# Run-time expert tiles of a MoE kernel: order of turns, down products and weight splits written by hand

## The chip, the cores and the metric

One core of a Trainium2 chip runs the whole program. The metric is the device time of one execution in microseconds (us). TensorE does matrix products and transposes into PSUM, ScalarE and VectorE copy and compute between PSUM and SBUF, GpSimd issues the indirect transfers (gathers and scatters), SyncE issues the others.

## The reference

Three layers in sequence, in float32. Attention with rotary embedding (batch 4, 8 heads, 576 rows, head width 64); a dense layer with a SoLU activation and a layer norm (512 to 1024 to 512); and a routed layer, which is the one that matters here:

```
do_compute = (x @ w_skip) > 0            # 2304 rows of 512
e_idx  = argmax(x @ w_gate)              # 8 experts
h      = maximum(x @ w1[e], 0)           # 512 -> 1024
y      = gate_w * (h @ w2[e])            # 1024 -> 512
out    = x + y where do_compute, else x
```

## The kernel before, in words

Every float32 product is made of three products of split operands: a high part `h` and a low part `l` of each operand, as `hh`, `hl`, `lh`. So a product of a 128-row tile with a 512-wide half of `w1` is 4 row blocks (`kc`) x 3 = 12 matmuls of 128 x 512 (`up_mm`, L1077), both halves 24, and the product with `w2` is 8 blocks x 3 = 24 matmuls into one PSUM tile `ops` (`dn_mm`, L1098).

Attention, the dense layer, the routing and the first two expert tiles (`NEAR = 2`, of one expert that is chosen early) are put in order by a planner: a list scheduler with costs and priorities, whose result `g.emit` writes under a manual schedule. This part is the same in both kernels.

The other expert tiles come in a loop that is unrolled for the largest possible number of tiles (`NTL`), each iteration inside a run-time condition on the tile count (`n_t > t`, L1276). With these inputs six run; the texts call them the first to the sixth (last) dynamic tile; `u = t + 2` numbers all expert tiles. Rows sorted by expert are gathered 128 at a time. One iteration of the loop has these steps:

- `up_mm` and `relu` for each half `hf`: twelve matmuls into `hp`, then ScalarE writes `hs` (L1081).
- `gmeta(u + 3)`, `gather(u + 2)`: GpSimd asks for the row numbers (L1048) and the rows (L1058) of later tiles.
- `xp_t`, `xp_h`, `xp_l`: four transposes (L1065) of the next tile's rows, a high-part copy on ScalarE (L1068) and a low part on VectorE (L1071).
- a turn of each half of `hs`: four transposes (`tn_t`, L1085) into a `tp` tile, the high part `hh` on ScalarE (`tn_h`, L1088), the low part `hl` on VectorE (`tn_l`, L1092).
- 24 down products, `finish` (VectorE, `ys`, L1101) and `put` (GpSimd, the scatter to `out`, L1104).

Where a tile is the first of another expert, its weights are split. They have been loaded into `w1r` and `w2r` by SyncE; `split1` writes `w1h` (ScalarE, L966) and `w1l` (VectorE, L967) for one of 4 blocks of 128 x 1024, `split2` does `w2h` (L970) and `w2l` (L971) likewise. `change(t, parts)` loads a flag of the table `ct` into a register of each engine concerned and does this under a run-time condition (L1265, L1266); part 1 is w1, part 2 is w2 with `fetch` of the next expert's weights. The texts call such a condition a gate: load of the flag, compare-and-branch, the block, a jump. With these inputs only the fourth dynamic tile changes the expert. In the loop of before no manual schedule is set, so within an iteration the framework's scheduler decides where each engine's instructions go.

Of the kernel before, what the change touches and what calls it, by code (L numbers as in the profile page):

```python
# [264 lines left out]
def kern(ctx, tc, q, k, v, w_in, w_out, g_ln, w_skip, w_gate, w1, w2, cs, ids, out):  # L265
    nc = tc.nc
    P = 128
# [7 lines left out]
    KC = DM // P  # L275
    FC = FF // P
# [11 lines left out]
    half = cst.tile([P, 1], F32, name="half")  # L288
# [674 lines left out]
    m = {}  # L963

    def split1(kc, raw):
        nc.scalar.activation(m["w1h"][:, kc], raw, AF.Copy)  # L966
        nc.vector.tensor_tensor(m["w1l"][:, kc], raw, m["w1h"][:, kc].bitcast(F32), op=ALU.subtract)  # L967

    def split2(kc, raw):
        nc.scalar.activation(m["w2h"][:, kc:kc + 2], raw, AF.Copy)  # L970
        nc.vector.tensor_tensor(m["w2l"][:, kc:kc + 2], raw, m["w2h"][:, kc:kc + 2].bitcast(F32), op=ALU.subtract)  # L971
# [73 lines left out]
    def gmeta(u):  # L1045
        mt = m["mt"][u % 5]
        r = erw[:, u:u + 1] if u < NEAR else m["rows"][:, u - NEAR:u - NEAR + 1]
        nc.gpsimd.indirect_dma_start(out=mt, out_offset=None, in_=srt[:, :],  # L1048
                                     in_offset=bass.IndirectOffsetOnAxis(ap=r, axis=0),
                                     bounds_check=E * REG - 1, oob_is_err=False)  # L1050
# [5 lines left out]
    def gather(u):  # L1056
        src, top = (out[0:2 * S], 2 * S) if u < NEAR else (out, NT)
        return nc.gpsimd.indirect_dma_start(  # L1058
            out=m["xr"][u % 3], out_offset=None, in_=src[:, :],
            in_offset=bass.IndirectOffsetOnAxis(ap=m["mt"][u % 5][:, 1:2].bitcast(I32), axis=0),  # L1060
            bounds_check=top - 1, oob_is_err=False)

    def xp_t(u, tp):
        for k_ in range(KC):
            nc.tensor.transpose(tp[:, k_ * P:(k_ + 1) * P], m["xr"][u % 3][:, k_ * P:(k_ + 1) * P], ident)  # L1065

    def xp_h(u, tp):
        nc.scalar.activation(m["xh"][u % 2], tp, AF.Copy)  # L1068

    def xp_l(u, tp):  # L1070
        nc.vector.tensor_tensor(m["xl"][u % 2], tp, m["xh"][u % 2].bitcast(F32), op=ALU.subtract)  # L1071

    def up_mm(u, hf, kc, h):
        xh, xl = m["xh"][u % 2], m["xl"][u % 2]
        fs, ks = slice(hf * 512, hf * 512 + 512), slice(kc * P, kc * P + P)
        for y, (a, bb) in enumerate(((xh, "w1h"), (xh, "w1l"), (xl, "w1h"))):
            nc.tensor.matmul(h, lhsT=a[:, ks], rhs=m[bb][:, kc, fs], start=(kc == 0 and y == 0),  # L1077
                             stop=(kc == KC - 1 and y == 2))

    def relu(hf, h):  # L1080
        nc.scalar.activation(m["hs"][:, hf * 512:hf * 512 + 512], h, AF.Relu)  # L1081

    def tn_t(hf, tp):
        for k_ in range(4):
            nc.tensor.transpose(tp[:, k_ * P:(k_ + 1) * P], m["hs"][:, (4 * hf + k_) * P:(4 * hf + k_ + 1) * P], ident)  # L1085

    def tn_h(hf, tp):
        nc.scalar.activation(m["hh"][:, hf * 512:hf * 512 + 512], tp, AF.Copy)  # L1088

    def tn_l(hf, tp):  # L1090
        fs = slice(hf * 512, hf * 512 + 512)
        nc.vector.tensor_tensor(m["hl"][:, fs], tp, m["hh"][:, fs].bitcast(F32), op=ALU.subtract)  # L1092

    DOWN = [(a, bb, kc) for a, bb in (("hh", "w2h"), ("hh", "w2l"), ("hl", "w2h")) for kc in range(FC)]

    def dn_mm(i, ob):
        a, bb, kc = DOWN[i]
        nc.tensor.matmul(ob, lhsT=m[a][:, kc * P:kc * P + P], rhs=m[bb][:, kc], start=(i == 0), stop=(i == len(DOWN) - 1))  # L1098

    def finish(u, ob):  # L1100
        nc.vector.scalar_tensor_tensor(m["ys"][u % 2], ob, m["mt"][u % 5][:, 0:1], m["xr"][u % 3], op0=ALU.mult, op1=ALU.add)  # L1101

    def put(u):
        nc.gpsimd.indirect_dma_start(  # L1104
            out=out, out_offset=bass.IndirectOffsetOnAxis(ap=m["mt"][u % 5][:, 1:2].bitcast(I32), axis=0),
            in_=m["ys"][u % 2], in_offset=None, bounds_check=NT - 1, oob_is_err=False)
# [96 lines left out]
    for kc in range(KC):  # L1203
        for hf in range(2):
            i = 2 * kc + hf
# [24 lines left out]
    for u in range(NEAR):  # L1230
        x = 102 + 10 * u
# [12 lines left out]
    rows, ct = m["rows"], m["ct"]  # L1244

    def fetch(reg, after=None):
        for i in range(2):
            d = [nc.sync.dma_start(m["w1r"][:, 2 * i:2 * i + 2], w1v(reg & (E - 1))[:, 2 * i:2 * i + 2], cond=reg < SL)]
            d += [nc.sync.dma_start(m["w2r"][:, 4 * i:4 * i + 4], w2v(reg & (E - 1))[:, 4 * i:4 * i + 4], cond=reg < SL)]
            if after is not None:  # L1250
                for x in d:
                    tc.add_manual_dep(x.ins, after.ins.name, mybir.DependencyInfo(mybir.DependencyClass.Sync, mybir.DependencyReason.DATA), reason="rows first")
# [6 lines left out]
    hps = [[pm.tile([P, 512], F32, name=f"hp{i}{j}") for j in range(2)] for i in range(2)]  # L1259
    tps = [pm.tile([P, 512], F32, name=f"tp{i}") for i in range(3)]  # L1260
    ops = pm.tile([P, 512], F32, name="ops")

    def change(t, parts):
        engs = [mybir.EngineType.Activation, mybir.EngineType.DVE] + [mybir.EngineType.SP] * (parts >> 1)
        new = nc.values_load(ct[0:1, 0, t:t + 1], engines=engs, min_val=0, max_val=1)  # L1265
        with tc.If(new > 0):  # L1266
            if parts & 1:
                for kc in range(KC):
                    split1(kc, m["w1r"][:, kc])
            if parts & 2:  # L1270
                for kc in range(0, FC, 2):
                    split2(kc, m["w2r"][:, kc:kc + 2])
                fetch(nc.sync.value_load(ct[0:1, 1, t:t + 1], min_val=0, max_val=SL))

    change(0, 3)
    with ExitStack() as nest:  # L1276
        for t in range(NTL):
            nest.enter_context(tc.If(n_t > t))
            u = t + NEAR
            if t:  # L1280
                change(t, 2)
            for hf in range(2):
                for kc in range(KC):
                    up_mm(u, hf, kc, hps[u % 2][hf])
                relu(hf, hps[u % 2][hf])
            gmeta(u + 3)
            gather(u + 2)
            xp_t(u + 1, tps[0])
            xp_h(u + 1, tps[0])
            xp_l(u + 1, tps[0])  # L1290
            for hf in range(2):
                tn_t(hf, tps[1 + hf])
                tn_h(hf, tps[1 + hf])
                tn_l(hf, tps[1 + hf])
            if t + 1 < NTL:
                change(t + 1, 1)
            for i in range(len(DOWN)):
                dn_mm(i, ops)
            finish(u, ops)
            put(u)  # L1300

# [41 lines left out]
```

## Time and profile before

| | us |
|---|---|
| median of 3 runs | 689.01 (686.5 to 692.22) |
| profiled execution | 688.96 |
| its span | 687.2 |
| TensorE busy | 634.6 (92%) |
| VectorE busy | 483.7 (70%) |
| ScalarE busy | 372.7 (54%) |
| GpSimd busy | 259.6 (38%) |

The span is the time from the first to the last instruction that the profiler saw in one execution; 1.76 us of that execution lie around it. Busy shares are averages over stages with different limits. The loop of dynamic tiles takes the stretch from 593.84 to 677.15 us of the span, 83.31 us. Starts and ends of matmuls overlap because they are pipelined; the step from one start to the next is the time that one costs.

### The profile page before, as it was taken

What the parts mean: (1) busy time and instruction counts of PE and PEld (TensorE: products, weight loads), DVE (VectorE), ACT (ScalarE), POOL (GpSimd) and SP (SyncE); (2) the same over time, 40 slices, a digit from 0 to 9 for tenths busy, and PEclk for the clock granted to TensorE, in tenths of its full rate; (3) what the DMA queues carried; (4) which work ended last, traced back from release to release, by engine and by line L of the source; (5) the groups of instructions that cost most, each with busy time, mean ns of one, the idle gap of its engine ahead of it and who ended that gap; (6) DMA issues with size and microseconds to landing.
All of it is one profiled execution on the core that took longest, in us unless ns stands there. A gap on an engine that the chain in (4) does not pass through costs nothing. (4 is left out here: it accounts for less than half of the span.)

```text
span 687.2 us, 12857 instructions
## 1 busy us (share of the span) xinstructions
PE 634.6 (92%) x4588; PEld 483.6 (70%) x4588; DVE 483.7 (70%) x1199; ACT 372.7 (54%) x899; POOL 259.6 (38%) x278
## 2 busy tenths in 40 slices
PE   2597989989999999999999999999999989898993
PEld 1465766767777787777777777777877767677772
DVE  5588798898678788687886975868569857124411
ACT  2687798776557575854556754565335421123321
POOL 5776369463343633243333243112020422321330
PEclk9998999989999999999999999999999999999998
DMA  4633344431212331124222012100134211541000
GB/s 129 169 98 114 85 143 144 116 96 62 64 36 65 83 84 34 38 65 81 69 37 64 12 36 50 35 17 1 22 108 117 78 46 26 188 151 32 18 32 11
DMA packets 42187, 49.10 MB, mean 71 GB/s; under 512 B 27508, under 2 KB 27636, under 8 KB 42112
## 3 DMA queue, kind: packets, MB, share of 16 engines
q1 hardware_dynamic: 39744, 44.43, 24.3%
q0 software_dynamic: 2368, 3.74, 1.8%
q8 instruction: 38, 0.62, 0.4%
q14 instruction: 37, 0.30, 0.1%
HBM read 38.50 MB, written 6.99 MB: 66 GB/s over the span
## 5 line engine op out<-in xcount | busy, mean ns | idle before, releaser
L624 ACT ACTIVATE P<-S,nm 128x576 f32<-128x576 f32 x144 | 106.7, 742 | 45.5 <-DVE nm L621 44.2
L621 DVE TENSOR_REDUCE nm<-S 128x1 f32<-128x576 f32 x144 | 106.8, 748 | 12.3 <-PE S L618 11.6
L847 PE MATMUL A<-woh,lh 128*128 128x512 f32 x288 | 108.0, 416 | 0.0
L618 PE MATMUL S<-k,qa 64*128 64x288 f32 x576 | 96.5, 322 | 5.3 <-ACT P L624 3.2
L724 PE MATMUL T<-ptall,vt 128*64 128x256 f32 (+2 forms) x960 | 92.9, 337 | 0.8 <-DVE qa L558 0.8
L685 PE MATMUL T<-ident,P 128*128 128x128 f32 x576 | 87.9, 285 | 5.9 <-ACT ptall L692 2.0
L647 POOL TENSOR_SCALAR P<-P,sr 128x576 f32<-128x576 f32 x57 | 45.8, 809 | 111.2 <-DVE sr L633 94.7
L618 PE MATMUL S<-k,qb 64*128 64x288 f32 x384 | 81.4, 333 | 5.1 <-ACT P L624 5.1
L685 PEld LDWEIGHTS T<-ident,P 128*128 128x128 f32 x576 | 67.6, 145 | 24.2 <-issue 6.9
L618 PEld LDWEIGHTS S<-k,qa 64*128 64x128 f32 x576 | 70.4, 192 | 17.7 <-ACT P L624 6.5
L724 PEld LDWEIGHTS T<-ptall,vt 128*64 128x64 f32 (+1 forms) x960 | 55.7, 138 | 30.9 <-issue 6.5
L692 ACT ACTIVATE ptall<-T 128x512 f32<-128x512 f32 (+1 forms) x110 | 51.2, 491 | 37.2 <-PE T L685 36.8
L618 PEld LDWEIGHTS S<-k,qb 64*128 64x128 f32 x384 | 57.3, 196 | 16.6 <-ACT P L624 7.6
L847 PEld LDWEIGHTS A<-woh,lh 128*128 128x128 f32 x288 | 54.4, 189 | 12.3 <-issue 2.1
L772 PE MATMUL S<-wih,xth 128*128 128x512 f32 x144 | 60.7, 422 | 0.1
L772 PE MATMUL S<-wih,xtl 128*128 128x512 f32 x144 | 56.6, 393 | 0.0
L847 PE MATMUL A<-wol,lh 128*128 128x512 f32 x144 | 56.5, 392 | 0.0
L772 PE MATMUL S<-wil,xth 128*128 128x512 f32 x144 | 56.3, 391 | 0.0
L498 POOL TENSOR_TENSOR rt<-raw,csq 128x576 f32<-128x576 f32 x24 | 34.8, 1452 | 55.2 <-PE T L529 36.1
L694 DVE COPY ptall<-T 128x512 f32<-128x512 f32 (+1 forms) x82 | 44.2, 552 | 11.8 <-PE T L685 11.3
L801 POOL TENSOR_TENSOR st<-st,half 128x1 f32<-128x1 f32 x18 | 10.7, 595 | 79.6 <-DVE st L798 47.0
L923 POOL DMA_INDIRECT srt<-gi,ix x18 | 19.5, 1085 | 55.1 <-DVE sc L893 13.7
(228 smaller groups left out, 1302.3 us busy)
## 6 DMA issues: line engine op xcount, KB each, us to landing
qb<-qa SPq DMA_DIRECT2D x30, 256.0 KB, 3.8
raw<-in_q SPq DMA_DIRECT2D x16, 288.0 KB, 3.2
raw<-in_k SPq DMA_DIRECT2D x16, 288.0 KB, 3.1
out<-xs SPq DMA_DIRECT2D x36, 128.0 KB, 2.7
s<-in_moe_w_in SPq DMA_DIRECT2D x8, 512.0 KB, 4.9
s<-in_moe_w_out SPq DMA_DIRECT2D x8, 512.0 KB, 3.4
st<-in_moe_w SPq DMA_DIRECT2D x8, 512.0 KB, 3.7
w1r<-in_moe_w SPq DMA_DIRECT2D x4, 1024.0 KB, 8.0
```

Source lines behind the costliest of these rows:

```text
L498: e.tensor_tensor(t1[:, 0:NJ].rearrange("p j (e i) -> p j e i", e=2), raw.t.rearrange("p j (e i) -> p j e i", e=2), c, op=ALU.mult)
L618: nc.tensor.matmul(sp[:, bank, 0:288], lhsT=l, rhs=r_, start=first, stop=fin)
L621: nc.vector.tensor_reduce(nm[:, x:x + 1], sp.t[:, :, 0:288], AX.XY, ALU.max, negate=True)
L624: nc.scalar.activation(pt[:, x * S:(x + 1) * S].rearrange("p (a b) -> p a b", a=2), sp.t[:, :, 0:288], AF.Exp, bias=nm[:, x:x + 1], accum_ ...
L647: nc.gpsimd.tensor_scalar(y, y, sr[:, x:x + 1], 1.0, op0=ALU.mult, op1=ALU.mult)
L685: nc.tensor.transpose(tp.t[:w_, (y - g0) * P:(y - g0) * P + P], pt[:, y * P:y * P + w_], ident)
L692: nc.scalar.activation(ov, iv, AF.Copy)
L694: nc.vector.tensor_copy(ov, iv)
L724: nc.tensor.matmul(xp.t[64 * h:64 * h + 64, 0:M], lhsT=l, rhs=r_, start=(i == 0), stop=(i == 4))
L772: nc.tensor.matmul(hp[:, hf], lhsT=a, rhs=bb, start=(kc == 0 and y == 0), stop=(kc == KC - 1 and y == 2))
L847: nc.tensor.matmul(ob.t, lhsT=lh[:, a, kc], rhs=bb[:, kc], start=(kc == 0 and y == 0), stop=(kc == FC - 1 and y == 2))
L923: nc.gpsimd.indirect_dma_start(out=srt[:, :], out_offset=bass.IndirectOffsetOnAxis(ap=ix[:, 0:1], axis=0), in_=gi.t, in_offset=None, bound ...
```

## The change

The loop gets a manual schedule, so each engine's instructions stand in the order in which the code lists them. The first turn stands inside the second up product, after two of its four row blocks. The down products are listed with the four blocks of `hh` and `hl` from the first half first (12 products), then the other 12; four of them stand ahead of the second turn, the rest behind it. The split of w1 for the next tile stands behind the second turn, and that of w2 in two blocks, one ahead of the first up product and one behind the first relu; each block has a gate of its own, with one flag load per tile.

```diff
--- before.py
+++ after.py
@@ -1260,42 +1260,64 @@
     tps = [pm.tile([P, 512], F32, name=f"tp{i}") for i in range(3)]
     ops = pm.tile([P, 512], F32, name="ops")
 
-    def change(t, parts):
-        engs = [mybir.EngineType.Activation, mybir.EngineType.DVE] + [mybir.EngineType.SP] * (parts >> 1)
-        new = nc.values_load(ct[0:1, 0, t:t + 1], engines=engs, min_val=0, max_val=1)
-        with tc.If(new > 0):
-            if parts & 1:
-                for kc in range(KC):
-                    split1(kc, m["w1r"][:, kc])
-            if parts & 2:
-                for kc in range(0, FC, 2):
-                    split2(kc, m["w2r"][:, kc:kc + 2])
+    AD = [mybir.EngineType.Activation, mybir.EngineType.DVE, mybir.EngineType.SP]
+    new = {}
+
+    def change1(t):
+        new[t] = nc.values_load(ct[0:1, 0, t:t + 1], engines=AD, min_val=0, max_val=1)
+        with tc.If(new[t] > 0):
+            for kc in range(KC):
+                split1(kc, m["w1r"][:, kc])
+
+    def change2(t, half):
+        with tc.If(new[t] > 0):
+            for kc in range(4 * half, 4 * half + 4, 2):
+                split2(kc, m["w2r"][:, kc:kc + 2])
+            if half:
                 fetch(nc.sync.value_load(ct[0:1, 1, t:t + 1], min_val=0, max_val=SL))
 
-    change(0, 3)
-    with ExitStack() as nest:
+
+    first = [i for i in range(len(DOWN)) if DOWN[i][2] < 4]
+    order = first + [i for i in range(len(DOWN)) if DOWN[i][2] >= 4]
+    AHEAD = 4
+
+    def down(part):
+        for x in part:
+            a, bb, kc = DOWN[x]
+            nc.tensor.matmul(ops, lhsT=m[a][:, kc * P:kc * P + P], rhs=m[bb][:, kc], start=(x == order[0]),
+                             stop=(x == order[-1]))
+
+    def turn(hf):
+        tn_t(hf, tps[1 + hf])
+        tn_h(hf, tps[1 + hf])
+        tn_l(hf, tps[1 + hf])
+
+    change1(0)
+    with tc.manual_schedule(), ExitStack() as nest:
         for t in range(NTL):
             nest.enter_context(tc.If(n_t > t))
             u = t + NEAR
-            if t:
-                change(t, 2)
-            for hf in range(2):
-                for kc in range(KC):
-                    up_mm(u, hf, kc, hps[u % 2][hf])
-                relu(hf, hps[u % 2][hf])
+            change2(t, 0)
+            for kc in range(KC):
+                up_mm(u, 0, kc, hps[u % 2][0])
+            relu(0, hps[u % 2][0])
+            change2(t, 1)
+            for kc in range(KC // 2):
+                up_mm(u, 1, kc, hps[u % 2][1])
+            turn(0)
+            for kc in range(KC // 2, KC):
+                up_mm(u, 1, kc, hps[u % 2][1])
+            relu(1, hps[u % 2][1])
             gmeta(u + 3)
             gather(u + 2)
             xp_t(u + 1, tps[0])
             xp_h(u + 1, tps[0])
             xp_l(u + 1, tps[0])
-            for hf in range(2):
-                tn_t(hf, tps[1 + hf])
-                tn_h(hf, tps[1 + hf])
-                tn_l(hf, tps[1 + hf])
+            down(order[:AHEAD])
+            turn(1)
             if t + 1 < NTL:
-                change(t + 1, 1)
-            for i in range(len(DOWN)):
-                dn_mm(i, ops)
+                change1(t + 1)
+            down(order[AHEAD:])
             finish(u, ops)
             put(u)
 
```

TensorE, second dynamic tile, from the last up product on. `hp_6593` is the second half's PSUM tile, `tp_6594` that of the next rows, `tp_6595` and `tp_6596` those of the two turns. Before:

```order
L1077 MATMUL hp_6593<-w1h,xl_6095 128x512
L1065 MATMUL tp_6594<-ident,xr_6104 128x128
L1266 UNCONDITIONAL_BRANCH
L1065 MATMUL tp_6594<-ident,xr_6104 128x128 x3
L1085 MATMUL tp_6595<-ident,hs 128x128 x4
L1085 MATMUL tp_6596<-ident,hs 128x128 x4
L1098 MATMUL ops<-w2h,hh 128x512 x8
L1098 MATMUL ops<-w2l,hh 128x512 x8
L1098 MATMUL ops<-w2h,hl 128x512 x8
```

Now, from the last product of the second row block of the second half on:

```order
L1077 MATMUL hp_6593<-w1h,xl_6095 128x512
L1085 MATMUL tp_6595<-ident,hs 128x128 x4
L1077 MATMUL hp_6593<-w1h,xh_6093 128x512
L1077 MATMUL hp_6593<-w1l,xh_6093 128x512
...
L1077 MATMUL hp_6593<-w1h,xl_6095 128x512
L1065 MATMUL tp_6594<-ident,xr_6104 128x128 x4
L1287 MATMUL ops<-w2h,hh 128x512 x4
L1085 MATMUL tp_6596<-ident,hs 128x128 x4
L1287 MATMUL ops<-w2l,hh 128x512 x4
L1287 MATMUL ops<-w2h,hl 128x512 x2
L1268 UNCONDITIONAL_BRANCH
```

The first turn has moved ahead of six up products, four down products stand between the transposes of the next rows and the second turn, and a jump stands among the down products instead of among the transposes.

ScalarE, second dynamic tile, from the first relu (`hs` from `hp_6592`) on. L1266, L1268 and L1273 are gates. Before:

```order
L1081 ACTIVATE hs<-hp_6592 128x512
L1266 COMPARE_AND_BRANCH
L966 ACTIVATE w1h<-w1r 128x1024 x4
L1266 UNCONDITIONAL_BRANCH x2
L1081 ACTIVATE hs<-hp_6593 128x512
L1068 ACTIVATE xh_6092<-tp_6594 128x512
L1088 ACTIVATE hh<-tp_6595 128x512
L1088 ACTIVATE hh<-tp_6596 128x512
```

Now:

```order
L1081 ACTIVATE hs<-hp_6592 128x512
L1273 COMPARE_AND_BRANCH
L970 ACTIVATE w2h<-w2r 128x1024 x2
L1273 UNCONDITIONAL_BRANCH x2
L1088 ACTIVATE hh<-tp_6595 128x512
L1081 ACTIVATE hs<-hp_6593 128x512
L1068 ACTIVATE xh_6092<-tp_6594 128x512
L1088 ACTIVATE hh<-tp_6596 128x512
L1267 TENSOR_LOAD ct
L1268 COMPARE_AND_BRANCH
L966 ACTIVATE w1h<-w1r 128x1024 x4
L1268 UNCONDITIONAL_BRANCH x2
```

Between the two relus stood the gated split of w1. Now the gated second block of w2 and the first high-part copy stand there, and the gated split of w1 has moved behind the second high-part copy.

VectorE, second dynamic tile, from the gated split of w1 on. Before:

```order
L1265 TENSOR_LOAD ct
L1266 COMPARE_AND_BRANCH
L967 TENSOR_TENSOR w1l<-w1r,w1h 128x1024 x4
L1266 UNCONDITIONAL_BRANCH x2
L1071 TENSOR_TENSOR xl_6094<-tp_6594,xh_6092 128x512
L1092 TENSOR_TENSOR hl<-tp_6595,hh 128x512
L1092 TENSOR_TENSOR hl<-tp_6596,hh 128x512
L1101 SCALAR_TENSOR_TENSOR ys_6100<-ops,mt_6109,xr_6103 128x512
L1276 COMPARE_AND_BRANCH
```

Now, from the first low part of the turn on:

```order
L1092 TENSOR_TENSOR hl<-tp_6595,hh 128x512
L1071 TENSOR_TENSOR xl_6094<-tp_6594,xh_6092 128x512
L1092 TENSOR_TENSOR hl<-tp_6596,hh 128x512
L1267 TENSOR_LOAD ct
L1268 COMPARE_AND_BRANCH
L967 TENSOR_TENSOR w1l<-w1r,w1h 128x1024 x4
L1268 UNCONDITIONAL_BRANCH x2
L1101 SCALAR_TENSOR_TENSOR ys_6100<-ops,mt_6109,xr_6103 128x512
L1296 COMPARE_AND_BRANCH
L1273 COMPARE_AND_BRANCH
```

The split of w1 stood ahead of the three low parts; it now stands behind them and ahead of the tile's output `ys`.

## Rows read from the trace of the kernel before

**Rows 1.** The page: busy time, share, instructions of TensorE; granted clock in 40 slices.
```profile
PE 634.6 (92%) x4588; PEld 483.6 (70%) x4588; DVE 483.7 (70%) x1199; ACT 372.7 (54%) x899; POOL 259.6 (38%) x278
...
PEclk9998999989999999999999999999999999999998
```

**Rows 2.** Chain of waits, second dynamic tile: start us, length us, what.
```profile
609.25 5.59 PE hp L1077 x24
...
615.23 0.61 ACT hs L1081
...
616.86 5.86 PE ops L1098 x24
```

**Rows 3.** Windows, six stretches: length, TensorE busy (count), granted clock, DMA, GB/s.
```profile
601.55:603.38 1.83, 1.51 (x14) 1.00 1.02 412
614.68:616.86 2.18, 1.69 (x13) 1.00 0.42 124
628.16:631.72 3.56, 1.69 (x13) 1.00 0.27 74
643.03:644.91 1.88, 1.56 (x13) 1.00 0.13 16
656.21:658.10 1.89, 1.57 (x14) 1.00 0.02 0
669.40:671.29 1.89, 1.57 (x14) 1.00 0.02 0
sum 13.23, PE 9.60; mean PE 1.60
```

**Rows 4.** Timeline, last tile: start, length, engine, line, work, [idle before, releaser].
```profile
663.80 0.39 PE L1077 MATMUL hp<-w1h,xh 128*128 128x512 f32 x1
...
666.86 0.60 ACT L1081 ACTIVATE hs<-hp 128x512 f32<-128x512 f32 x1 [8.33 <-PE hp L1077]
...
669.40 0.60 PE L1065 MATMUL tp<-ident,xr 128*128 128x128 f32 x4
...
669.83 1.14 PE L1085 MATMUL tp<-ident,hs 128*128 128x128 f32 x8
...
671.29 2.13 PE L1098 MATMUL ops<-w2h,hh 128*128 128x512 f32 x8 [0.32 <-ACT hh L1088]
...
673.26 2.03 PE L1098 MATMUL ops<-w2l,hh 128*128 128x512 f32 x8
```

**Rows 5.** Timeline, third tile: the split of w1 on ScalarE and VectorE.
```profile
626.31 3.91 ACT L966 ACTIVATE w1h<-w1r 128x1024 fp32r<-128x1024 f32 x4
...
627.40 4.63 DVE L967 TENSOR_TENSOR w1l<-w1r,w1h 128x1024 fp32r<-128x1024 f32 x4 [3.89 <-ACT w1h L966]
```

**Rows 6.** Timeline, entry of the loop: VectorE and TensorE.
```profile
593.03 0.69 DVE L1071 TENSOR_TENSOR xl<-T,xh 128x512 fp32r<-128x512 f32 x1 [0.31 <-ACT xh L1068]
...
593.87 0.47 PE L1077 MATMUL hp<-w1h,xh 128*128 128x512 f32 x1 [1.50 <-DVE xl L1071]
594.54 0.50 PE L1077 MATMUL hp<-w1l,xh 128*128 128x512 f32 x1 [0.20 <-DVEq L1266]
```

**Rows 7.** Timeline, planned stage: four transposes and the products behind them.
```profile
574.18 0.64 PE L1085 MATMUL T<-ident,hs 128*128 128x128 f32 x4
...
574.57 0.48 PE L1077 MATMUL S<-w1h,xh 128*128 128x512 f32 x1
...
574.89 0.39 PE L1077 MATMUL S<-w1l,xh 128*128 128x512 f32 x1
```

**Rows 8.** Timeline, second tile: its first two up products.
```profile
609.09 0.39 PE L1077 MATMUL hp<-w1h,xh 128*128 128x512 f32 x1
...
609.32 0.40 PE L1077 MATMUL hp<-w1l,xh 128*128 128x512 f32 x1
```

**Rows 9.** Timeline, second tile: the second relu.
```profile
615.23 0.60 ACT L1081 ACTIVATE hs<-hp 128x512 f32<-128x512 f32 x1 [2.48 <-PE tp L1065]
```

**Rows 10.** Window in the first tile, columns as in Rows 3.
```profile
595.00:599.00 4.00, 4.00 (x13) 0.57 0.97 351
```

## The prediction

> **What bounds the kernel now.** I read the page first, then the chain of waits of the last 85 us, then the timeline of the tiles that the change touches. The page says that TensorE is busy 92% of the span at a granted clock of 0.8 or more in every slice [rows 1]; most of the program is a planned stage that the change leaves alone, so only the six run-time expert tiles near the end matter. There the chain is one engine: up products back to back, then a link through ScalarE (a relu, a transpose, a high-part copy), then 24 down products [rows 2]. So the tiles are bound by TensorE, and each has one hole, between its last up product and its first down product.
>
> How large that hole is, a table of the six stretches from the transposes of the next rows to the first down product shows: 13.23 us in sum, 1.83 to 2.18 in five tiles and 3.56 in the third [rows 3]. The timeline of the last tile gives the prices. 24 up products take 669.40 - 663.80 = 5.60 us, 0.2333 each; four transposes take 669.83 - 669.40 = 0.43 us [rows 4]. Every stretch holds twelve transposes, 1.30 us of work. Six times 1.30 is 7.80, so 13.23 - 7.80 = 5.43 us are waiting and switching. The third tile has most of it because the split of the next expert's first matrix stands on ScalarE ahead of the second relu and runs 3.91 us there, from 626.31 to 630.22 [rows 5].
>
> **The change, part by part.** I put a tile's first up product at time 0.
>
> *First turn inside the second up product.* TensorE reaches the turn after 18 products, at 4.20. The relu that it needs starts at 666.86 - 663.80 = 3.06 and takes 0.60 [rows 4], so it is over at 3.66: no wait. The work is moved, not added: 4 transposes.
>
> *Down product split round the second turn.* The other six up products end at 6.24 (six more intervals after the turn at 4.20 to 4.63, and a switch of 0.05, below). The second relu then runs from about 6.34 to 6.94. Meanwhile TensorE has the transposes of the next rows (6.08 to 6.51) and four down products (to 7.49), and only then asks for that relu's result: 0.55 us of cover. Those four products need the first high-part copy; the transposes for it end at 4.80, so it is there at 5.5 if the gate of the new second weight block, ahead of it on ScalarE, lets it through. What a gate costs, the loop's entry shows: VectorE's last work ends at 593.72 and TensorE is released by the gate's end at 594.54, so 0.82 us [rows 6]. The relu's end at 3.66 plus 0.82 is 4.48, before the transposes end. Twenty down products are left at 7.97, and the tile ends at 12.64, against 7.49 + 1.97 + 16 x 0.2333 = 13.19 in the last tile of before [rows 4].
>
> *More switches between transposes and products.* A tile has three where it had one in that stretch. In the planned stage four transposes and the product behind them take 574.89 - 574.18 = 0.71 us, 0.05 more than 0.43 + 0.233 [rows 7]. Upper bound: the first eight down products after the turn take 1.97 us where eight take 1.87, so 0.10 [rows 4]; lower bound nothing, since the transposes' own time is counted already. Eighteen switches cost 0.9 us (0 to 1.8).
>
> *One jump more on TensorE in each tile.* The first two up products of the second tile have a jump between them in the program's order and stand 609.32 - 609.09 = 0.23 us apart, like products without one [rows 8]. So I price it at nothing; the cover is TensorE's queue, and a jump that empties it is the slower rival below. [...]
>
> *Split of w1 after the second turn.* It leaves ScalarE's path to the second relu, and that is already in the 5.43. In exchange it starts late. In the third tile the second high-part copy ends at about 8.8, a gate of 0.82 follows, ScalarE starts at 9.6, VectorE 1.09 later, and VectorE's 4.63 us [rows 5] end at 15.4. TensorE starts the fourth tile at 12.64 and wants the last block's low part with its eleventh product, at 14.97: a new stall of about 0.4 us. Behind it on VectorE waits the third tile's output, some 2.5 us later than now, and on GpSimd its store; the sum's PSUM tile is wanted again only 6.5 us into the next tile, so nobody on the path waits.
>
> *w2 in two blocks.* The first block (half of 3.9 us) is over before the fourth tile's first relu is due. The second stands between that relu and the first high-part copy: relu over at 3.66 after that tile's start, two splits of 0.98, a gate of at most 0.8, so the copy is there at about 7.0, where TensorE wants it at 6.5. I take 0.6. Both expert stalls together: 1.0 us, from 0 (short gates) to 2.5, if each gate is as long as the 2.48 us that ScalarE once stood idle with a gate inside [rows 9].
>
> *Queues.* SyncE asks for the next expert only behind the second block, some us later; no tile after the fourth changes its expert, so nobody waits. GpSimd's metadata load, gather and store keep their order, only the jumps between them move.
>
> **The sum.** 5.43 - 0.9 - 1.0 = 3.5 us gained (bounds 5.43 and 5.43 - 1.8 - 2.5 = 1.1). The profiled execution took 688.96 us, a span of 687.2 and 1.8 around it, and lies on the median of the three runs, 689.01. So 688.96 - 3.5 = 685.5, which is 0.5% less; a measurement of this kernel tells about 1% (6.9 us) from no change.
>
> **Rivals.**
> *Slower: gates become the path.* On ScalarE a gate now stands between the first relu and the first high-part copy in every tile. TensorE wants that copy at 6.5, so a gate may last until 5.9 - 3.66 = 2.2 us for nothing. Above that every us costs six. For it: one wait of 2.48 with a gate inside [rows 9]. Against it: 0.82 measured [rows 6]. The gain is gone at 2.2 + 3.5 / 6 = 2.8 us; at 4 us the time is 688.96 - 3.5 + 6 x 1.8 = 696. Chance 0.09. [...]
>
> *No change: the hole moves.* The expert stalls and switches come at their upper bounds, 688.96 - 1.1 = 688. For it: the third and fourth tiles have long ScalarE and VectorE work in a row with little room. Against: these are two tiles of six. Here belongs also that it doesn't do what it says, because a turn waits elsewhere: then 689. Chance 0.16.
>
> [...] Chance 0.09. [...]
>
> **Numbers.** Forecast 0.66, with its own range of 684 to 687.5. Range for 8 in 10: from 681.5, the fastest rival less some scatter, to 690, the no-change rival and scatter of about 1.5 us (the three runs lie 2.5 below to 3.2 above their median). Above it lies most of the slower rival. Faster by over 1% (below 682.1): half of the fastest rival and a little scatter, 0.08. Slower by over 1% (above 695.9): most of the gate rival, 0.08. Within 1%: 0.84.
>
> **What would show it.** Right: the tiles start 12.6 to 12.8 us apart instead of 13.2 to 14.9; no TensorE wait for the second relu or the second high-part copy; waits of under 1 us at the fourth tile's start for the w1 low part and in its middle for the first high-part copy. Wrong: TensorE idle in every tile before its first down products, with ScalarE's gate as releaser; transposes that cost over 0.1 us per switch; a stall of over 2 us in the fourth tile; or a stretch at half clock somewhere in the later tiles, which a TensorE that waits less should not have.

## The result and the profile after

The changed kernel takes 682.58 us, median of 6 runs (680.67 to 684.96); in the same comparison the kernel before takes 690.75 (686.5 to 692.22). The ratio is 0.989 with a 95% interval from 0.9852 to 0.9928. A second comparison gave 0.9894 (0.9869 to 0.9918). So the change makes the kernel about 1.1% faster, 8 us by the medians, where 3.5 were forecast.

The profiled execution took 684.35 us, with a span of 682.0. The page of the changed kernel, busy times and granted clock, to be read beside [rows 1]:

```profile
PE 632.5 (93%) x4588; PEld 483.2 (71%) x4588; DVE 484.5 (71%) x1199; ACT 373.7 (55%) x899; POOL 259.5 (38%) x278
...
PEclk9998999979999999999999999999999989999997
```

TensorE does the same number of instructions and is busy for 632.5 us instead of 634.6; the span is 5.2 us shorter. Digits below 9 stand in other places of the clock's row. The chain of waits shows the loop best. Here is one tile of it, the second (start us, length us, what), where [rows 2] had a relu in the chain:

```profile
609.21 4.20 PE hp L1077 x18
613.41 0.44 PE tp L1085 x4
613.85 1.40 PE hp L1077 x6
615.25 0.44 PE tp L1065 x4
615.68 0.94 PE ops L1287 x4
616.62 0.44 PE tp L1085 x4
617.05 4.66 PE ops L1287 x20
621.71 4.20 PE hp L1077 x18
```

Nothing but TensorE is left in the chain: 18 up products, the first turn, 6 up products, the transposes of the next rows, 4 down products, the second turn, 20 down products, and the next tile. The windows from one first up product to the next (length, TensorE busy with the count of records, granted clock, DMA share, GB/s), behind a window at the loop's entry:

```profile
596.68:601.00 4.32, 4.32 (x20) 1.00 0.95 355
609.05:621.55 12.50, 12.50 (x61) 1.00 0.15 45
621.55:634.05 12.50, 12.50 (x61) 1.00 0.14 43
634.05:646.55 12.50, 12.50 (x61) 1.00 0.08 24
646.55:659.05 12.50, 12.50 (x61) 1.00 0.07 24
```

Four tiles of 12.50 us, TensorE busy for 12.50 of each, also the third (621.55 to 634.05) and the fourth, in which the expert changes. That is the price of the work alone: 48 x 0.2333 + 1.30 = 12.50. The holes of [rows 3] are gone to the last tenth. The entry ran at full clock in this execution, where [rows 10] has 0.57.

ScalarE and VectorE at the change of expert, on their own timelines (start, length, engine, line, work, idle before and its releaser):

```profile
629.64 0.60 ACT L1088 ACTIVATE hh<-tp 128x512 fp32r<-128x512 f32 x1 [0.70 <-ACT xh L1068]
630.21 3.91 ACT L966 ACTIVATE w1h<-w1r 128x1024 fp32r<-128x1024 f32 x4
...
637.11 0.60 ACT L1081 ACTIVATE hs<-hp 128x512 f32<-128x512 f32 x1 [1.09 <-PE hp L1077]
637.61 2.00 ACT L970 ACTIVATE w2h<-w2r 128x1024 fp32r<-128x1024 f32 x2
639.51 0.58 ACT L1088 ACTIVATE hh<-tp 128x512 fp32r<-128x512 f32 x1
```

```profile
631.30 4.63 DVE L967 TENSOR_TENSOR w1l<-w1r,w1h 128x1024 fp32r<-128x1024 f32 x4 [0.34 <-ACT w1h L966]
635.85 0.74 DVE L1101 SCALAR_TENSOR_TENSOR ys<-ops,mt,xr 128x512 f32<-128x512 f32 x1
```

The split of w1 starts at 630.21, when the second high-part copy ends (629.64 + 0.60), although a gate lies between them. The second block of w2 follows the first relu in the same way, at 637.61. What became of the gate, the instructions of ScalarE's sequencer (`q` behind the engine) in the third tile show: how often, duration in ns (min/median/max), first and last start in us.

```profile
L1267 ACTq TENSOR_LOAD <-ct x1: 274/274/274, 629.7 to 629.7; - x1
L1268 ACTq COMPARE_BRANCH  x1: 40/40/40, 630.0 to 630.0; - x1
```

The load of the flag and the compare-and-branch are done while the copy (629.64 to 630.24) still runs, so nothing of them is left between the copy and the split. The third tile's output `ys` on VectorE waits for the split, until 635.85 (in the other tiles it comes right behind the last down product), and nobody waits for it.

The single profiled executions can't be set against each other as wholes. The first up product of the loop comes at 593.87 in the one of before and at 596.00 in the one of after, although what lies ahead of it is the same program; in all fourteen profiles of this study it comes between 590.63 and 596.35. So I compare the loop, from its first up product to the end of its last down product: 83.28 us before, 75.71 after.

### The profile page after: what moved, and what is told of

Read it like the earlier page. It is cut to its first block, busy times and chain, and to the rows that moved or that the text cites. A ratio compares the mean times of both kernels' runs of the same rounds, so it can differ in the third digit from the quotient of the medians.

```text
span 682.0 us, 12882 instructions
## 1 busy us (share of the span) xinstructions
PE 632.5 (93%) x4588; PEld 483.2 (71%) x4588; DVE 484.5 (71%) x1199; ACT 373.7 (55%) x899; POOL 259.5 (38%) x278
## 5 line engine op out<-in xcount | busy, mean ns | idle before, releaser
L847 PEld LDWEIGHTS A<-woh,lh 128*128 128x128 f32 x288 | 54.3, 189 | 12.8 <-issue 2.1
```

Of the source, the lines that this page charges most:

```text
L847: nc.tensor.matmul(ob.t, lhsT=lh[:, a, kc], rhs=bb[:, kc], start=(kc == 0 and y == 0), stop=(kc == FC - 1 and y == 2))
```

## The experiments

Theory A: the gain is the hole between the last up and the first down product, closed by the early turn, the cover of four down products, and the split of w1 taken off the path to the second relu. Its rivals: the manual schedule itself does it (B), or a part of the change is not needed. Behind it stands the question why the medians moved by more than the holes.

**The schedule alone.** The loop of before, with one line changed, so that each engine takes the old listing's order:

```diff
-    with ExitStack() as nest:
+    with tc.manual_schedule(), ExitStack() as nest:
```

> The loop of before with a manual schedule and nothing else: turns, down products and gates in the old listing's order. Theory A (the gain is the hole between the last up and the first down product, closed by the early turn and the four down products; the schedule itself only takes the split of w1 off the third tile): all six tiles stay at about 13.2 us with a TensorE wait of about 0.3 us for the high-part copies in each; only the third tile falls from 14.87 to 13.2, so the loop gets 1.7 to 2.0 us shorter than before, far from the 5.4 us of the change. Theory B (the manual schedule does most of it, by where it puts gates and jumps): tiles near 12.5 us and most of the gain here.

TensorE's timeline of the fourth tile's first down product, and the first up products of the fifth and sixth tile:

```profile
643.88 2.13 PE L1098 MATMUL ops<-w2h,hh 128*128 128x512 f32 x8 [0.32 <-ACT hh L1088]
...
649.59 0.39 PE L1077 MATMUL hp<-w1h,xh 128*128 128x512 f32 x1
...
662.78 0.40 PE L1077 MATMUL hp<-w1h,xh 128*128 128x512 f32 x1
```

662.78 - 649.59 = 13.19, and 0.32 us of wait for the high-part copy, in every tile. All four periods after the first are 13.19 or 13.20, the third tile's included, and the loop takes 79.79 us, 3.5 less than before: 2.0 by the third tile (14.87 to 13.19) and the second (13.47 to 13.19), the rest because its entry ran at full clock in this execution. So theory B falls: the listed order takes the w1 split off the third tile's path, and not much more. The ratio, however, was 0.9947 (0.9928 to 0.9966), some 3.7 us. That gap over 2.0 comes up again below.

**The changed kernel again.** No edit; compared with the kernel before as the schedule alone was.

> The changed kernel once more. Theory A: tiles of 12.50 us each again, to 0.02 us, since nothing but TensorE's own work is left in them; the time 5 to 6 us under before on the mean of executions, with a scatter of about 2 us either way that goes with the granted clock. Theory C (the 8 us between the medians are the change's own): about 8 us again, whatever the clock did, and the slow stretch at the loop's entry is gone for good in this kernel.

683.58 us against 691.28, ratio 0.9894, and tiles of 12.50 four times. But the entry is slow this time (clock 0.70 over the first 5 us, as against 0.66 in the first profile of before), and the loop takes 77.25 us instead of 75.71. So theory C is right on the 8 us and falls on the entry. Theory A is right on the tiles; the 7.7 us between the medians are more than its 5 to 6, but the interval (5.7 to 9.1 us) reaches down to it.

**No cover for the second relu.**

```diff
-    AHEAD = 4
+    AHEAD = 0
```

> AHEAD = 0: no down product between the transposes of the next rows and the second turn; all 24 behind it. Theory A: TensorE reaches the second turn 0.93 us earlier, at about 6.48 us of the tile, and waits for the second relu (over at 6.74, seen at 6.8): a wait of about 0.3 us, tiles of 12.8 us, in all six; that is what the four products cover. Theory B': the cover isn't needed, tiles stay at 12.50.

The transposes of the next rows and the second turn, fourth tile:

```profile
639.50 0.60 PE L1065 MATMUL tp<-ident,xr 128*128 128x128 f32 x4
640.42 0.66 PE L1085 MATMUL tp<-ident,hs 128*128 128x128 f32 x4 [0.31 <-ACT hs L1081]
```

0.31 us of wait for the relu, as expected, in all six tiles (0.25 to 0.32). But the tiles are 13.04 us, 0.54 more and not 0.3. The idle time that the profile names is counted from ends that are modelled, and these lie behind the start of the next instruction where nothing waits (0.39 us long, the next start 0.23 us on, in [rows 8]). Counted from starts, the turn begins 640.42 - 639.50 = 0.92 us after four transposes that take 0.43, so nearly 0.5 us are lost there. The four products are worth 0.5 us a tile.

**The first turn late.**

```diff
-            for kc in range(KC // 2):
-                up_mm(u, 1, kc, hps[u % 2][1])
-            turn(0)
-            for kc in range(KC // 2, KC):
+            for kc in range(KC):
                 up_mm(u, 1, kc, hps[u % 2][1])
...
             xp_l(u + 1, tps[0])
+            turn(0)
             down(order[:AHEAD])
```

> The first turn behind the transposes of the next rows instead of inside the second up product, all else as in the change. Theory A: the first four down products now wait for the first high-part copy, which stands behind the second relu and the next rows' copy on ScalarE and is over at about 7.5 us of the tile where TensorE could start at 6.5: about 1.0 us of wait, tiles of 13.5 us, worse than before's 13.2. Theory D (the split of the down product alone closes the hole): tiles under 12.8.

The first down products of the fourth tile:

```profile
644.43 0.73 PE L1287 MATMUL ops<-w2h,hh 128*128 128x512 f32 x2 [0.85 <-ACT hh L1088]
```

0.85 us of wait for the first high-part copy, tiles of 13.63 us, worse than before's 13.19. The split of the down product needs the early turn; theory D falls.

**Twelve switches per tile.** The twelve transposes singly, one ahead of each of four up products and eight down products (parts of the edit, `...` stands for the rest):

```diff
-            turn(0)
...
+                    if n < 4:
+                        tr(tps[1], m["hs"], n)
...
-            xp_t(u + 1, tps[0])
+            for k_ in range(4):
+                tr(tps[0], m["xr"][(u + 1) % 3], k_)
+                down(order[k_:k_ + 1])
```

> The change with its twelve transposes per tile put singly between products: twelve switches from a transpose to a product per tile instead of three, same work. Theory A (a switch costs nothing on a TensorE that doesn't wait; the 0.10 us seen before is the restart after a wait): tiles of 12.50 us. The price of the record, 0.05 us a switch: 12.95 us; its upper bound, 0.10: 13.4 us.

First up products of the third and fourth tile; between them, from the third tile, a transpose of the next rows, the down product behind it, and the next two transposes; at the end two products of the fourth:

```profile
620.03 0.40 PE L1077 MATMUL hp<-w1h,xh 128*128 128x512 f32 x1
...
626.05 0.27 PE L1306 MATMUL tp<-ident,xr 128*128 128x128 f32 x1
626.26 0.51 PE L1287 MATMUL ops<-w2h,hh 128*128 128x512 f32 x1
626.61 0.27 PE L1306 MATMUL tp<-ident,xr 128*128 128x128 f32 x1
...
626.95 0.27 PE L1306 MATMUL tp<-ident,xr 128*128 128x128 f32 x1
...
632.75 0.39 PE L1077 MATMUL hp<-w1h,xh 128*128 128x512 f32 x1
...
635.38 0.50 PE L1077 MATMUL hp<-w1l,xh 128*128 128x512 f32 x1 [0.15 <-DVE w1l L967]
635.71 0.39 PE L1077 MATMUL hp<-w1h,xl 128*128 128x512 f32 x1
```

ScalarE's first high-part copy in the third tile:

```profile
625.61 0.60 ACT L1088 ACTIVATE hh<-tp 128x512 fp32r<-128x512 f32 x1 [1.93 <-PE tp L1306]
```

The second, third and fifth tile take 12.70 to 12.72 us, 0.20 to 0.22 more, but the switches don't cost this. A transpose and a product take 626.95 - 626.61 = 0.34 us, which is 0.11 and 0.23: a switch costs nothing. Only the first such pair takes longer, 626.61 - 626.05 = 0.56. The turn's transposes end later when they stand between products, so the copy runs until 626.21, and the first down product starts at 626.26, when it is over. The profile names no wait there, because it counts from the modelled end of the transpose. So theory A holds for the switch, and the 0.2 us are a wait for the copy that the edit makes.

The fourth tile takes 13.12 us: the second turn ends later, with it starts the split of w1, and TensorE waits for its low part. So the room that the split has in the changed kernel is a few tenths of a us. The product behind that wait also shows a restart: the next one starts 635.71 - 635.38 = 0.33 us after it, 0.10 more than usual, with no transpose near.

**Eight more gates.**

```diff
             change2(t, 1)
+            for i in range(8):
+                with tc.If(new[t] > 0):
+                    nc.scalar.activation(m["tb"][:, 8], m["tb"][:, 0], AF.Copy)
```

> The change with eight more gates (without a flag load, a tiny ScalarE copy inside that runs in the fourth tile only) between the first relu and the first high-part copy. If a gate costs ScalarE 0.82 us as at the loop's entry: 8 x 0.82 = 6.6 us after the relu's end at 3.7, the copy ends near 11 where TensorE wants it at 6.5, tiles of about 17 us. Theory A (the sequencer resolves a gate in some 0.1 to 0.2 us once the flag is in a register): 0.8 to 1.6 us, the copy still starts when its transposes end, tiles of 12.50 to 12.9 us.

ScalarE's first high-part copy of the third tile, which follows the first relu and the gates:

```profile
624.77 0.60 ACT L1088 ACTIVATE hh<-tp 128x512 fp32r<-128x512 f32 x1 [2.09 <-ACTq L1306]
```

2.09 us for nine gates, 0.23 each, where in the changed kernel it was 1.23 us of waiting for TensorE's transposes. Here nothing ran on ScalarE that could hide them. The second and third tile take 12.53 us. (In the fourth the eight copies run, 1.93 us, and TensorE waits 1.44; why the fifth takes 12.81 stays open.) So nine gates in a row that skip their block cost 0.03 us a tile. A gate of 0.1 to 0.2 us, as theory A has it, is near what the trace of the changed kernel shows, where ScalarE's compare-and-branches behind the third tile's split (L1268, L1296, L1273) take 34 to 40 ns and start at 630.6, 630.7 and 630.8 us; the 0.23 here are a little more. These eight skip one small copy each; that gates which skip a whole split cost nothing either, the tiles of 12.50 of the changed kernel show. The slower rival is out.

**The split of w1 back ahead of the second relu.**

```diff
+            if t + 1 < NTL:
+                change1(t + 1)
             relu(1, hps[u % 2][1])
...
-            if t + 1 < NTL:
-                change1(t + 1)
             down(order[AHEAD:])
```

> The change with the gated split of w1 on ScalarE ahead of the second relu, where before had it, instead of behind the second turn. Theory A: nothing in the five tiles without a split (12.50 us), since the gate fits into ScalarE's idle time; in the third tile the second relu comes some 3.9 us after the first high-part copy, at 9.8 to 10.6 us of the tile instead of 6.7, and TensorE, which has cover up to 7.5, waits 2.6 to 3.2 us: 15.1 to 15.7 us for that tile. Rival: the split of w1 behind the turn is what costs, and the third and fourth tiles together get shorter here.

ScalarE in the third tile, then TensorE's second turn there, then two windows of TensorE behind it (columns as above; the third number from the end is the clock):

```profile
621.08 0.60 ACT L1088 ACTIVATE hh<-tp 128x512 fp32r<-128x512 f32 x1 [1.23 <-PE tp L1085]
621.65 3.91 ACT L966 ACTIVATE w1h<-w1r 128x1024 fp32r<-128x1024 f32 x4
625.46 0.58 ACT L1081 ACTIVATE hs<-hp 128x512 f32<-128x512 f32 x1
```

```profile
626.09 0.65 PE L1085 MATMUL tp<-ident,hs 128*128 128x128 f32 x4 [2.33 <-ACT hs L1081]
```

```profile
626.09:627.00 0.91, 0.91 (x6) 1.00 0.00 0
627.50:630.50 3.00, 3.00 (x8) 0.50 0.00 0
```

The second relu stands behind 3.91 us of split, and TensorE waits 2.33 us. The second, fourth and fifth tile stay at 12.50. But the third takes 16.60, so the rival falls: the third and fourth together get longer. It is also 0.9 more than the upper end expected: 1.4 us behind the wait TensorE runs at 0.50 of its clock for some 3.4 us. This slow stretch had not been part of any theory for a tile inside the loop.

**The kernel before, three more times.** No edit; only to see where its time goes.

> The kernel before, profiled once more. Its profile so far (span 687.2 us) lies at the short end of its executions (spans of 686.7 to 691.8), so it may lack something that most have. Theory A (slow-clock stretches of 3 to 4 us fall at other places in each execution and are the whole scatter): the loop takes 81.6 or 83.3 us, without or with such a stretch at its entry, tiles as before (13.5, 14.9, 13.2, 13.2, 13.2), and the planned stage holds the rest of the difference. Theory E (the loop of before loses more in most executions, in its third tile or in a gate): the loop takes 85 us or more, with the loss at one named wait.

TensorE in the third tile: the second turn, then windows over the eight first down products and the rest of the tile:

```profile
629.17 0.66 PE L1085 MATMUL tp<-ident,hs 128*128 128x128 f32 x4 [1.56 <-ACT hs L1081]
```

```profile
630.15:633.66 3.51, 3.51 (x8) 0.51 0.14 55
633.66:637.39 3.73, 3.73 (x17) 1.00 0.00 0
```

Eight products that take 1.97 us in [rows 4] take 3.51 here, at 0.51 of the clock: 1.54 us lost, and the third tile takes 16.41 us instead of 14.87. The entry ran at full clock this time. The loop takes 83.28 us, as in the first profile. So theory E falls, and theory A fails on its tiles: the stretch lay not at the entry but in the third tile. Theory F is made from these two profiles: the third tile's wait in the kernel before can be followed by a stretch at half clock, as here, which costs it about 1.5 us more in part of its executions, and the changed kernel has no such wait.

> The kernel before, a third profile. In the second one TensorE's wait of 1.56 us in the third tile was followed by 3.4 us at half clock, in the first one the wait at the loop's entry was. [...] Theory A alone: such stretches come anywhere, also in tiles without a wait of over 1 us.

Slow at the entry (clock 0.66 over the first 5 us), third tile 14.86, loop 83.30.

> The same once more, for the count. Theory F: of all profiles with a third tile that waits 1.5 us or more (four of before, one of the change with the split ahead of the second relu) at least two show the half clock there, and of the profiles without it (the changed kernel's two, the schedule alone, no cover, turn late, twelve switches) none does. Theory A alone: no difference between the two groups.

Slow in the third tile (16.40), not at the entry, loop 83.30. So each of the four profiles of before has one slow stretch in its loop, two at the entry and two behind the third tile's wait. All eight slow stretches in the loops of the fourteen profiles begin behind a wait of TensorE of 1.5 us or more. Of the five profiles with a wait of over 1.5 us in the third tile (these four and the kernel above) three have it there, and of the nine without such a wait there none; the entry, whose wait is the same in thirteen of the fourteen, has it in five. Theory F held; but two of the three (this kernel's second profile and the one above) are those it was made from, and the two profiles taken for it gave one of two.

**w2 in one block.** `change2` does all four splits of w2 at once (the edit's part in the loop):

```diff
-            change2(t, 0)
+            change2(t)
...
-            change2(t, 1)
```

> The change with w2 in one block of four, ahead of the first up product. Only the fourth tile can differ. ScalarE's w1 split is over about 0.2 us before the tile starts minus nothing to spare, so four splits of 0.98 end at about 3.9 us of the tile, where the first relu is due at 3.06: the relu is over at 4.4 instead of 3.7, and the first turn at 4.2 waits 0.2 us: 12.7 us. What the two blocks give is then 0.2 us. Rival (the two blocks carry the transition): over 1 us of wait in the fourth tile.

ScalarE from the w2 block to the first high-part copy of the fourth tile:

```profile
630.19 3.90 ACT L970 ACTIVATE w2h<-w2r 128x1024 fp32r<-128x1024 f32 x4
633.99 0.58 ACT L1081 ACTIVATE hs<-hp 128x512 f32<-128x512 f32 x1
635.36 0.60 ACT L1088 ACTIVATE hh<-tp 128x512 fp32r<-128x512 f32 x1 [0.80 <-ACT hs L1081]
```

The block ends at about 634.0 and the relu starts there, 0.7 us after its products are done; TensorE's fourth tile takes 12.77 us and the others 12.50. The two blocks are worth 0.27 us in a call with one change of expert.

**The entry.** What is left is in front of the loop, so the transposes of the first tile's rows were put four planned down products earlier:

```diff
             op("PE", "mm1", lambda i=i: dn_mm(i, ob.t), r=[...], w=[(ob, 0)], pri=pri,
+               after=[m["x4"]] if u == NEAR - 1 and i >= 20 else [])
```

> The change, and in the planned stage the transposes of the first dynamic tile's rows four down products earlier, so that their copies run beside those products. Theory A: the rows have landed by then, so TensorE waits nothing there; at the loop's entry the wait for the next rows' low part (1.5 us) goes, and what is left is the gate, which starts when VectorE has written the last planned output: the second up product comes about 0.6 us sooner after the last planned product than in the change. 0.1% in time, under what the measurement can tell. Rival: the rows land later than the 20th product, and TensorE waits inside the down product for as long as it gains at the entry.

TensorE at the entry, in the changed kernel and here:

```profile
592.03 2.03 PE L1098 MATMUL A<-w2h,hl 128*128 128x512 f32 x8
...
596.00 0.47 PE L1077 MATMUL hp<-w1h,xh 128*128 128x512 f32 x1 [1.50 <-DVE xl L1071]
596.68 0.50 PE L1077 MATMUL hp<-w1l,xh 128*128 128x512 f32 x1 [0.20 <-DVEq L1268]
```

```profile
591.00 1.10 PE L1098 MATMUL A<-w2h,hl 128*128 128x512 f32 x4
592.01 0.66 PE L1065 MATMUL T<-ident,xr 128*128 128x128 f32 x4
...
594.83 0.47 PE L1077 MATMUL hp<-w1h,xh 128*128 128x512 f32 x1 [1.23 <-DVE ys L1101]
595.15 0.50 PE L1077 MATMUL hp<-w1l,xh 128*128 128x512 f32 x1
```

From the first of the last eight planned down products to the second up product it is 596.68 - 592.03 = 4.65 us in the changed kernel and 595.15 - 591.00 = 4.15 here. The wait is now 1.23 us, for VectorE and its gate. The ratio to before is 0.9886 (0.9857 to 0.9915), which can't be told from the change's own; by the trace this is the best version, by 0.5 us.

## Why the prediction was right, and where its sizes were off

*The bound and the hole: right.* TensorE bound the tiles, the hole was where it was said to be, and the listed parts close it: with cover and early turn the tiles are 12.50, without the one 13.04, without the other 13.63. The tiles were forecast at 12.6 to 12.8. The mechanism was right; three sizes were off, and that the time lies in the stated range is in part luck, because the lower end of that range was set for another reason, the loss of the slow start.

*Switches, 0.9 us: mis-sized, and of the wrong sign.* The 0.10 us that the first eight products behind a wait take longer [rows 4] were read as an upper bound for a switch. Where TensorE doesn't wait a switch costs nothing: three leave the tile at 12.50, and of twelve a pair of transpose and product takes 0.34 us, as much as the two alone. What the 0.10 belongs to is the restart after the wait (0.33 between two products there, without a transpose), and it goes with the wait. The forecast's own tiles, 13.19 and 12.64, hold these 0.10, but its sum doesn't: by the tiles it would have been 6 x 0.55, 1.68 and 0.28 for the third and second tile, less the 1.0 for the expert, 4.3 us. Between two profiles with the same slow entry, before and the second one of the changed kernel (whose loop takes 77.25), the loop is 83.28 - 77.25 = 6.03 us shorter: the 5.43 of the table and six times 0.10.

*Expert stalls, 1.0 us: nothing.* The step that failed is the gate of 0.82 us from the loop's entry [rows 6], which was put behind each piece of work in the loop. At the entry VectorE's flag load takes 0.56 us:

```profile
L1265 DVEq TENSOR_LOAD <-ct x1: 557/557/557, 593.6 to 593.6; - x1
```

It starts only about 0.1 us before VectorE's last work ends (593.72), so most of it lies open. Why it takes twice the 0.27 us of the load in the third tile isn't shown. Inside the loop a gate costs ScalarE 0.23 us if nothing runs beside it, and the split of w1 begins as the copy ahead of it ends. With this the low part is there at 631.30 + 4.63 = 635.93, and the eleventh product wants it at 634.05 + 10 x 0.2333 = 636.38: 0.45 us of room instead of a stall of 0.4. The first high-part copy of the fourth tile is over at 640.09, 6.04 us after the tile's start, where 7.0 was forecast and TensorE wants it at 6.5.

*Jumps on TensorE, nothing: right.* Tiles of 12.50 us, all of it products and transposes, leave no room for them. TensorE's queue ran ahead: the 65 ns compare-and-branch that admits the second tile starts at 604.9 us in the trace of before, 4.2 us ahead of that tile's first product at 609.09 [rows 8]; in the changed kernel the one for the third tile starts at 618.5, 3.0 us ahead of 621.55. A jump that empties this queue was not shown in any run, and the slower rival is worked out for ScalarE's gates alone. There a gate took 0.23 us in the row of nine, with whatever belongs to one.

*The slow start: wrong.* The forecast counted the slow stretch at the loop's entry [rows 10] again, because the change moves nothing ahead of it, and so took it for a property of the place. The entry has it in 5 of 13 profiles with the same wait. No run shows the 1.7 us that the fastest rival's sums took for it; it costs 1.55 us, and before had one in all four profiles, at the entry or in the third tile; loops with this entry and no wait of over 1 us inside had one in three of seven. With that, 4 of 7 times 1.55 is 0.9 us more for the change on average, an estimate from eleven profiles. That a TensorE that waits less should have no stretch at half clock in the later tiles was the author's guess; the tiles of 12.50 us show none. The schedule alone, which has no such wait either, can gain part of its time beyond the 2.0 in the same way.

*The sum.* 6.0 + 0.9 = 6.9 us, against 8.2 and 7.7 between the medians; the interval of the second comparison reaches from 5.7 to 9.1 us. What remains, about 1 us, isn't settled: it is inside the interval, and no loop in the profiles shows it, nor does what lies ahead of the loop (590.94 to 593.87 us in the four profiles of before, 593.86 and 596.00 in the two of the change). Part of the 8.2 is where the forecast started: at 688.96, while the median of before in this comparison is 690.75. From 688.96 the loop's 6.0 alone lead to 682.9. The measured 682.58 lies in the stated range, below the likeliest case's own (684 to 687.5), next to the 682.8 of the fastest rival, the slow start gone as well, which was given 0.09; but its ground, an entry at full clock for good, didn't come. The chance of 0.08 for over 1% looks too low, with two ratios of 0.989; both intervals reach beyond 0.99, so it isn't certain.

*The slower rival: out.* Gates would have had to grow from 0.23 to over 2.2 us. The wait of 2.48 us that spoke for it [rows 9] was mostly no gate: between two relus lie twelve products of 0.2333, 2.8 us, less 0.60 for the first relu.

## What to carry to other kernels

Price a hole on the busy engine by the distance between its neighbours minus the work inside, not by the wait that the profile names: of 0.7 us a tile here, 0.32 was named. Of the 18 waits of 1.5 us or more on TensorE in these loops, 8 were followed by a stretch at half clock that cost 1.55 us more, so such waits were worth more here than their length. Don't price a gate by one that stands at a stage's entry: it was 0.82 us there [rows 6], and in the loop it ran beside the work ahead of it, or took 0.23. And when executions scatter by more than the effect, compare the period of the repeated stage instead of the whole time of one execution; it held to 0.02 us here wherever the granted clock was full.

## What the runs showed of the hardware that was not expected

- Waits of TensorE of 1.5 to 2.3 us were followed by about 3.4 us at half clock in some executions and not in others of the same program: third tile 3 of 5 profiles (2 of the 4 of the kernel before), entry 5 of 13. One wait of 1.44 us, one of 1.23 and the waits of 0.3 to 0.9 us in each tile were not followed by one in any profile.
- Single transposes between products cost nothing beyond their own time on a TensorE that has no wait: 0.34 us for a transpose and a product, 0.11 and 0.23 apart.
- Gates on ScalarE cost 0.23 us each in a row of nine, and nothing where ScalarE still had work ahead of them: the flag load (0.27 us) and the branch ran beside that work.
